# A windowed-attention kernel with top-1 experts: scatters without mutual order, a reordered attention step, and loads on two queues

## The chip, the core and the metric

The kernel runs on one core of a Trainium2 chip. A core has a matrix engine (TensorE, PE), a vector engine (VectorE, DVE), an engine for activations (ScalarE, ACT), a general one (GpSimd, POOL) and SyncE (SP), which here only issues transfers. Each takes its instructions in order from a queue of its own; semaphores join them. Sixteen DMA engines move data for all of them. The metric is device microseconds of one execution, lower is better.

## The reference

Attention with a window of 32 positions to either side and eight global positions, over 8 batches of 8 heads, 576 positions of 64; then a layer of eight experts, each token going to one:

```
scores = scale * np.matmul(q, k.transpose(0, 1, 3, 2))
mask = np.abs(pos[:, None] - pos[None, :]) <= window
mask = mask | is_global[:, None] | is_global[None, :]
...
x = attn_out.transpose(0, 2, 1, 3).reshape(B * S, H * D)
logits = x @ w_gate
expert_idx = np.argmax(logits, axis=1)
...
for e in range(E):
    h = np.maximum(x[expert_idx == e] @ w1[e], 0.0)
    out[expert_idx == e] = gate_w[expert_idx == e, None] * (h @ w2[e])
```

## The kernel before

The order on each engine is that of the source, written out by hand (a manual schedule); a framework places the semaphores from what each instruction reads and writes. There are four stages.

*Setup.* q, k and v of batch 0 are loaded (`load_qk`, L136; `load_v`, L145, twelve transfers of 96 KB a batch), all from SP. GpSimd gathers the k, q and v rows of the global positions with 16 indirect transfers (L202, L207), then makes identity and masks. q and k are cast to 16 bits and transposed on TensorE (`cast_qk`, L283; `trans_qk`, L289); the global v rows are copied into the v tiles (`load_vg`, L152).

*Attention.* `for b in range(B)`, and in it six steps t of 48 rows in each half of the sequence. A step consists of `scores` (a mask matmul, L357, then L370), `exps` (ScalarE, L377), `pvs` (P·V, L388), `zs` (the softmax sums, L400), and `merge_x` and `merge_z` (L405), which add the 12 columns that overlap with the step before on VectorE (L415), copy the 8 new ones on ScalarE (L410) and sum the columns of the global queries (L417). The scores of the next step are computed ahead of the present one's last merge. Between the steps stand two other kinds of work: casts (GpSimd, at the start of batch b), transposes of q and k of batch b + 1, and the `Tail` of batch b − 1. A tail computes router logits (`gate`, L458; `logits`, L473), normalized 16-bit rows (`rows`, L494), the choice of expert and the slot (`route1`, `ranks`, `route2`), and at t = 5 writes the rows into a slot table in DRAM with six indirect transfers (`scatter`, L571). Tail pieces and transposes share a pool of two PSUM tiles (tag `tr`). After the last step `join` (GpSimd, L430) adds the seams of the two halves in place. In batches 1 to 4 two pieces of expert weights of 1 MB are loaded and cast on ScalarE at t = 3 and 4 (L590).

*End of attention.* The tail of batch 7, and one for the global rows of all batches (`tg`), run with nothing beside them, then seven scatters.

*Experts.* For each of eight: four blocks of 128 rows are gathered from the slot table (`gather`, L712, with a memset on VectorE ahead of it, L711), transposed (L732), multiplied by w1 (L832), passed through a ReLU on ScalarE and VectorE in turn (L747, L749), multiplied by w2 (L850), scaled (`yout`) and scattered to the output by indirect transfers (L742). Eight row buffers serve two experts. Weights come in pieces of 1 MB through two staging buffers (`wfetch`, L582, L585), and are cast on GpSimd, VectorE and ScalarE (L592, L590). `overflow_plan`, some 30 small VectorE operations in expert 1, works out which blocks are left over where an expert has more than 512 tokens; these run last, one by one (`ov_block`).

The framework orders all writes to the slot table among each other, and all writes to the output, since it can't see that the indices differ.

## Time and profile before

| | |
|---|---|
| median of three runs | 799.98 us (799.2 to 801.22) |
| the profiled execution | 797.85 us, span 795.8 |
| busy in the span: PE, PEld | 416.0, 251.0 us |
| busy: DVE, ACT, POOL | 260.1, 170.8, 230.6 us |
| mean granted TensorE clock | 0.794 of 2.4 GHz |
| moved by DMA | 83.91 MB, mean 105 GB/s |

PE is TensorE's matmuls, PEld its weight loads. "[18.79 <-POOL wall L283]" means that the engine was idle for 18.79 us before the instruction, and that the wait ended with what line 283 did on POOL. L and a number is a line of the kernel; a `q` behind an engine's name is its queue, where transfers are issued. A clock of 1.00 is 2.4 GHz, 0.50 is 1.2 GHz. Tiles carved out of the weights' memory all go by the name `wall`.

### The profile page before, as it was taken

How to read it: one execution, taken by the hardware profiler on the slowest of the kernel's cores; microseconds unless marked ns; L12 is line 12 of the kernel's file. 1: busy time of each engine (PE TensorE's matmuls, PEld its weight loads, DVE VectorE, ACT ScalarE, POOL GpSimd, SP SyncE). 2: the span in 40 equal slices, each digit the busy share in tenths (PEclk: the TensorE clock that was granted, in tenths of full speed). 3: DMA queues.
4: the chain of work that ended last, by engine and by line, in shares of the span. 5: the costliest groups of instructions: out<-in, count | busy, mean ns of one | idle time of the engine just before them, and what ended most of it. 6: DMA issues, size and time to landing. Idle time of an engine off the chain costs nothing. (4 is left out here: it accounts for less than half of the span.)

```text
span 795.8 us, 15839 instructions
## 1 busy us (share of the span) xinstructions
PE 416.0 (52%) x6583; PEld 251.0 (32%) x6583; DVE 260.1 (33%) x788; ACT 170.8 (21%) x270; POOL 230.6 (29%) x299
## 2 busy tenths in 40 slices
PE   0036874372572761753735423092763844769774
PEld 0024653251351540541523302041321421324331
DVE  1332253152251450440533424142522331423331
ACT  0033334142241250321221200021202202202121
POOL 5412211502503304116021031334143452543211
PEclk9999698587685785885886856587878868879998
DMA  9069584292471660820000000353636735421100
GB/s 189 11 131 172 88 224 87 60 234 41 103 196 39 157 144 27 161 42 20 2 16 17 7 25 20 143 169 135 227 112 213 255 125 208 166 66 69 65 23 28
DMA packets 74508, 83.91 MB, mean 105 GB/s; under 512 B 43772, under 2 KB 56716, under 8 KB 74432
## 3 DMA queue, kind: packets, MB, share of 16 engines
q1 hardware_dynamic: 64880, 63.46, 32.3%
q0 software_dynamic: 9008, 19.37, 7.5%
q8 instruction: 54, 0.88, 0.5%
q14 instruction: 22, 0.18, 0.1%
q10 hardware_dynamic: 544, 0.02, 0.0%
HBM read 68.10 MB, written 16.16 MB: 106 GB/s over the span
## 5 line engine op out<-in xcount | busy, mean ns | idle before, releaser
L832 PE MATMUL h<-xts,wall 128*128 128x512 f16 x256 | 71.8, 438 | 71.0 <-DVE ht L747 61.2
L289 PE MATMUL tr_qk<-idh,wall 96*128 96x96 f16 x384 | 28.0, 228 | 136.9 <-POOL wall L283 92.3
L388 PE MATMUL pv<-wall 56*64 56x128 f32 x1536 | 71.9, 336 | 22.6 <-issue 11.1
L571 POOL DMA_INDIRECT xslot_scr<-wall,si x25 | 24.9, 995 | 160.5 <-DVE wall L565 117.5
L388 PEld LDWEIGHTS pv<-wall 56*64 56x64 f32 x1536 | 56.5, 168 | 37.3 <-issue 19.1
L571 POOL DMA_INDIRECT xslot_scr<-x16x,si x24 | 23.8, 994 | 148.8 <-DVE x16x L565 90.5
L742 POOL DMA_INDIRECT out_dram<-y,xr x32 | 31.8, 993 | 116.3 <-DVE y L741 35.6
L289 PEld LDWEIGHTS <-wall 96*128 96x128 f16 x384 | 21.0, 109 | 140.0 <-POOL wall L283 93.0
L832 PEld LDWEIGHTS <-wall 128*128 128x128 f16 x256 | 27.6, 108 | 111.7 <-issue 89.4
L377 ACT ACTIVATE wall<-sc 128x1024 f32<-128x1024 f32 x48 | 49.1, 1023 | 59.6 <-PE sc L370 59.6
L850 PE MATMUL yp<-wall,ht 128*128 128x512 f16 x256 | 57.2, 381 | 2.4 <-DVE y L741 2.4
L410 ACT ACTIVATE xt<-pv 128x384 f32<-128x384 f32 x48 | 23.5, 490 | 133.2 <-PE pv L388 133.2
L462 DVE SCALAR_TENSOR_TENSOR lsb<-zt,tr_l 128x216 f32<-128x216 f32 x24 | 9.0, 373 | 126.3 <-PE tr_l L458 126.2
L415 DVE TENSOR_TENSOR xt<-xt,pv 128x576 f32<-128x576 f32 x40 | 30.2, 754 | 58.6 <-ACT xt L410 58.5
L749 ACT ACTIVATE ht<-h 128x512 f16<-128x512 f32 x32 | 18.7, 596 | 140.3 <-PE h L832 140.0
L283 POOL CAST wall<-wall 96x768 f16<-96x768 f32 x56 | 43.6, 818 | 8.9 <-DMA wall<-in_q_dram 5.3
L494 PE MATMUL tr_x<-id,xt 128*108 128x128 f32 x192 | 31.4, 313 | 24.2 <-ACT kt L294 22.3
L458 PE MATMUL tr_l<-xt,wgbd 128*32 128x216 f32 x192 | 18.1, 465 | 47.5 <-POOL xt L430 37.2
L400 PE MATMUL z<-wall,onesel 56*32 56x128 f32 x1536 | 40.0, 324 | 5.2 <-issue 5.2
L294 ACT ACTIVATE kt<-tr_qk 128x576 f16<-128x576 f16 x32 | 21.0, 656 | 100.0 <-PE tr_qk L289 100.0
L712 POOL DMA_INDIRECT xr<-xslot_scr,idx x32 | 35.3, 1103 | 16.6 <-issue 8.2
L850 PEld LDWEIGHTS <-ht 128*128 128x128 f16 x256 | 25.0, 99 | 31.4 <-issue 3.2
(225 smaller groups left out, 662.6 us busy)
## 6 DMA issues: line engine op xcount, KB each, us to landing
st<-in_moe_w_dram SPq DMA_DIRECT2D x24, 1024.0 KB
wall<-in_v_dram SPq DMA_DIRECT2D x96, 96.0 KB
wall<-in_moe_w_dram SPq DMA_DIRECT2D x8, 1024.0 KB
wall<-in_k_dram SPq DMA_DIRECT2D x7, 1152.0 KB
wall<-in_q_dram SPq DMA_DIRECT2D x7, 1152.0 KB
wall<-vg SPq DMA_DIRECT2D x16, 96.0 KB
wall<-in_k_dram SPq DMA_DIRECT2D x4, 288.0 KB
wall<-in_q_dram SPq DMA_DIRECT2D x4, 288.0 KB
```

Source lines behind the costliest of these rows:

```text
L283: eng.tensor_copy(o, i_)
L289: nc.tensor.transpose(out=ps[:, 96 * r : 96 * r + 96], in_=src[:, 768 * pair + 128 * r : 768 * pair + 128 * r + 128], identity=idh[0:96, 0 ...
L377: nc.scalar.activation(out=e.rearrange("p r c w -> p r (c w)"), in_=sc[:, :, 0 : 4 * WE], func=AF.Exp, scale=0.125)
L388: nc.tensor.matmul(out=pv[64 * r : 64 * r + 64, f, c * WE : (c + 1) * WE], lhsT=vt[ff, t, 64 * h : 64 * h + 64], rhs=e[ff, r, c, :], start ...
L400: nc.tensor.matmul(out=z[32 * c : 32 * c + 32, f, 0:WE], lhsT=onesel[ff, r, :], rhs=e[ff, r, c, :], start=(r == 0), stop=(r == 1))
L415: nc.vector.tensor_tensor(out=dl[:, :, :, o : o + 12], in0=dl[:, :, :, o : o + 12], in1=sl[:, :, :, 0:12], op=ALU.add)
L494: nc.tensor.transpose(out=ps[p, 128 * c : 128 * c + 128], in_=src, identity=id32)
L571: nc.gpsimd.indirect_dma_start(out=xslot, out_offset=IndirectOffsetOnAxis(ap=self.si[p, j : j + 1], axis=0), in_=self.x16[p, j, :].bitcast ...
L712: nc.gpsimd.indirect_dma_start(out=xr.bitcast(I16), out_offset=None, in_=xslot, in_offset=IndirectOffsetOnAxis(ap=ix, axis=0), bounds_chec ...
L742: nc.gpsimd.indirect_dma_start(out=out, out_offset=IndirectOffsetOnAxis(ap=xr[:, DM : DM + 2].bitcast(I32), axis=0), in_=y, in_offset=None ...
L832: nc.tensor.matmul(out=ps, lhsT=w1v[:, e, c, 128 * fb : 128 * fb + 128], rhs=xts[:, c, :], start=(c == 0), stop=(c == 3))
L850: nc.tensor.matmul(out=ps, lhsT=ht[:, fc, 128 * j : 128 * j + 128], rhs=w2v[:, e, fc, :], start=(fc == 0), stop=(fc == 7))
```

## The change

In the setup, identity and masks are made ahead of the gathers; twelve gathers replace 16 (v rows for two heads' halves land in 128 partitions and are copied to their place by two transfers), and the copy of the global v rows is issued ahead of the loads of batch 1. Constants of the routing are made after the first exp. Loads of q, and half of the v loads, are issued from ScalarE's queue; q sits in partitions 32 to 127, and its transposes have 128 columns. The columns of the global queries stand first in each block of scores; their sums over the steps are no longer kept by VectorE in each step, but copied by ScalarE with the new columns and added up once per batch (`sum_globals`). `merge_x` works in halves, which the two engines take in opposite order. In the step, the k transposes stand ahead of the scores, tail pieces and q transposes behind the exp in a new order, and the q loads at t = 4. Scatters to the slot table carry no order among each other, those of the output in the experts neither; the first gather waits for all scatters. The six scatters of a batch are issued one batch later, behind the casts. The overflow plan is cut into pieces of five operations between the ReLUs of expert 1. The diff, cut to its core:

```diff
-    def load_qk(b, pieces=1):
-        n = H // pieces
-        for i in range(pieces):
-            for dst, src in ((kf, k), (qf, q)):
-                nc.sync.dma_start(
-                    out=dst[:, 384 * n * i : 384 * n * (i + 1)].rearrange("p (h n) -> p h n", h=n),
-                    in_=src[b, n * i : n * (i + 1)].rearrange("h (p r) d -> p h (r d)", r=6))
+
+    def load_qk(b, which="kq"):
+        for i in range(4):
+            for w, dst, src, eng in (("k", kf, k, nc.sync), ("q", qf[32:128], q, nc.scalar)):
+                if w in which:
+                    eng.dma_start(
+                        out=dst[:, 768 * i : 768 * (i + 1)].rearrange("p (h n) -> p h n", h=2),
+                        in_=src[b, 2 * i : 2 * (i + 1)].rearrange("h (p r) d -> p h (r d)", r=6))
     def load_v(b):
         d = vb[b % 2]
         for t in range(NT):
             for f in range(2):
                 s0 = 288 * f + HW * t
-                nc.sync.dma_start(
+                (nc.scalar if f else nc.sync).dma_start(
                     out=d[64 * f : 64 * f + HW, t, :].rearrange("p (h d) -> p h d", h=H),
                     in_=v[b, :, s0 : s0 + HW, :].rearrange("h s d -> s h d"))
...
+
+    for dst, src in ((vgr, v), (kg, k), (qg, q)):
+        for i in range(4):
+            h = 4 * (i // 2) + i % 2
+            nc.gpsimd.indirect_dma_start(
+                out=dst[:, i, :], out_offset=None, in_=src.rearrange("b h s d -> (b h s) d"),
+                in_offset=IndirectOffsetOnAxis(ap=ridx[:, h : h + 1], axis=0),
+                bounds_check=B * H * S - 1, oob_is_err=False)
+    for s_ in range(2):
+        nc.sync.dma_start(out=vg.rearrange("p (u s r) d -> p u s (r d)", u=2, s=2)[:, :, s_],
+                          in_=vgr[64 * s_ : 64 * s_ + 64].rearrange("p (u r) d -> p u (r d)", u=2))
...
     def trans_qk(b, pair, which):
-        src = k16 if which == "k" else q16
         ps = trp.tile([128, 1024], FP16, tag="tr", name="tr_qk")
         for r in range(6):
-            nc.tensor.transpose(out=ps[:, 96 * r : 96 * r + 96], in_=src[:, 768 * pair + 128 * r : 768 * pair + 128 * r + 128],
-                                identity=idh[0:96, 0:96])
+            sl = slice(768 * pair + 128 * r, 768 * pair + 128 * r + 128)
+            if which == "q":
+                nc.tensor.transpose(out=ps[:, 128 * r : 128 * r + 128], in_=q16[:, sl], identity=idh)
+            else:
+                nc.tensor.transpose(out=ps[:, 96 * r : 96 * r + 96], in_=k16[:, sl], identity=idh[0:96, 0:96])
         if which == "q":
-            nc.vector.tensor_copy(qt[b % 2][:, pair, :, 6:102], ps[:, 0:S].rearrange("p (r a) -> p r a", r=R))
+            nc.vector.tensor_copy(qt[b % 2][:, pair, :, 6:102],
+                                  ps[:, 0:768].rearrange("p (r a) -> p r a", r=R)[:, :, 32:128])
...
-    def merge(t, src, n, dl, dg):
-
-        sl = src[:, :, 0:WQ].rearrange("p n (r a) -> p n r a", r=R)
-        sg = src[:, :, WQ:WE]
+    def merge(t, parts):
+
+
+
         o = 8 * t
-        nc.scalar.activation(out=dl[:, :, :, o + 12 : o + WP], in_=sl[:, :, :, 12:WP], func=AF.Copy)
-        if t == 0:
-            nc.vector.tensor_copy(dl[:, :, :, 0:12], sl[:, :, :, 0:12])
-            nc.vector.tensor_copy(dg, sg)
-        else:
-            nc.vector.tensor_tensor(out=dl[:, :, :, o : o + 12], in0=dl[:, :, :, o : o + 12],
-                                    in1=sl[:, :, :, 0:12], op=ALU.add)
-            nc.vector.tensor_tensor(out=dg, in0=dg, in1=sg, op=ALU.add)
+        new, old = [], []
+        for src, acc in parts:
+
+            sn = bass.AP(src.tensor, src.offset, [list(src.ap[0]), list(src.ap[1]), [WP, R + 1], [1, 8]])
+            new.append((acc[:, :, :, o + 12 : o + WP], sn))
+            old.append((acc[:, :, 1 : R + 1, o : o + 12],
+                        src[:, :, NG:WE].rearrange("p n (r a) -> p n r a", r=R)[:, :, :, 0:12]))
+        for i in range(len(parts)):
+            nc.scalar.activation(out=new[i][0], in_=new[i][1], func=AF.Copy)
+            d_, s_ = old[-1 - i]
+            if t == 0:
+                nc.vector.tensor_copy(d_, s_)
+            else:
+                nc.vector.tensor_tensor(out=d_, in0=d_, in1=s_, op=ALU.add)
 
     def merge_x(b, t, pv):
-        merge(t, pv.rearrange("p f (c w) -> p (f c) w", c=4), 8,
-              xt[b % 2].rearrange("p f c r a -> p (f c) r a"), xg[b % 2].rearrange("p f c g -> p (f c) g"))
+        merge(t, [(pv[:, f].rearrange("p (c w) -> p c w", c=4), xt[b % 2][:, f]) for f in range(2)])
 
     def merge_z(b, t, z):
-        merge(t, z[:, :, 0:WE], 2, zt[b % 2], zg[b % 2])
+        merge(t, [(z[:, :, 0:WE], zt[b % 2])])
...
+    def sum_globals(b):
+        x, z = xt[b % 2], zt[b % 2]
         s_ = slice(8 * b, 8 * b + 8)
-        nc.gpsimd.tensor_tensor(out=xtg[:, 0:4, s_], in0=xg[b % 2][:, 0], in1=xg[b % 2][:, 1], op=ALU.add)
-        nc.gpsimd.tensor_tensor(out=xtg[:, 4, s_], in0=zg[b % 2][:, 0], in1=zg[b % 2][:, 1], op=ALU.add)
+        for f in range(2):
+            nc.vector.tensor_reduce(out=gsum[:, f, 0:4], in_=x[:, f, :, 0, 12:XP].rearrange("p c (t g) -> p c g t", t=NT),
+                                    op=ALU.add, axis=AX.X)
+            nc.vector.tensor_reduce(out=gsum[:, f, 4], in_=z[:, f, 0, 12:XP].rearrange("p (t g) -> p g t", t=NT),
+                                    op=ALU.add, axis=AX.X)
+        nc.vector.tensor_tensor(out=xtg[:, :, s_], in0=gsum[:, 0], in1=gsum[:, 1], op=ALU.add)
...
         def scatter(self):
             p = slice(0, self.np)
             for j in range(self.nj):
-                nc.gpsimd.indirect_dma_start(
+                d_ = nc.gpsimd.indirect_dma_start(
                     out=xslot, out_offset=IndirectOffsetOnAxis(ap=self.si[p, j : j + 1], axis=0),
                     in_=self.x16[p, j, :].bitcast(I16), in_offset=None,
                     bounds_check=E * CAP - 1, oob_is_err=False)
+                tc.declare_no_dep(d_.ins, group="xslot", reason="every token has a slot of its own")
+                tc.add_to_no_dep_group("xslot", d_.ins)
+                scattered.append(d_.ins.name)
...
-    tail = None
+    routing_constants()
+    tail = done = None
     for b in range(B):
         if b + 1 < B:
             load_v(b + 1)
             load_vg(b + 1)
             for pair in range(4):
-                cast_qk(pair, nc.gpsimd)
-            fill_kg(b + 1)
+                cast_qk(pair, nc.gpsimd, nc.gpsimd)
+            fill_kg(b + 1, nc.gpsimd)
             if b + 2 < B:
-                load_qk(b + 2)
+                load_qk(b + 2, "k")
+        if done is not None:
+            done.scatter()
         if 1 <= b <= 7 and pre:
             wl = [pre.pop(0) for _ in range(min(2, len(pre)))]
             for i, p_ in enumerate(wl):
@@ -612,45 +660,53 @@
             wl = []
         for t in range(NT):
             n = NT * b + t
+            tr = t - 1 if b + 1 < B and 1 <= t <= 4 else None
             pv = pvs(b, t)
+            merge_x(b, t, pv)
             z = zs(b, t)
-            merge_x(b, t, pv)
+            merge_z(b, t, z)
+            if tr is not None:
+                trans_qk(b + 1, tr, "k")
             if n + 1 < NT * B:
                 nb, nt = divmod(n + 1, NT)
                 sc = scores(nb, nt)
                 exps(n + 1, sc)
-            merge_z(b, t, z)
-            if b + 1 < B and t < 5:
-                for pos in ((0,), (1,), (2, 3), (4, 5), (6, 7))[t]:
-                    trans_qk(b + 1, pos // 2, "kq"[pos % 2])
             if tail is not None:
-                if t == 0:
-                    tail.gate(0)
-                elif t == 1:
+                if t == 1:
                     tail.logits(0)
-                    tail.gate(1)
                 elif t == 2:
+                    tail.logits(1)
+                elif t == 3:
+                    tail.logits(2)
+                elif t == 4:
+                    tail.rows(1, 0)
+                    tail.ranks()
+                elif t == 5:
+                    tail.rows(2, 0)
+            if tr is not None:
+                trans_qk(b + 1, tr, "q")
+            if tail is not None:
+                if t < 3:
+                    tail.gate(t)
+                elif t == 3:
+                    tail.route1()
                     tail.rows(0, 0)
                     tail.rows(0, 1)
-                    tail.logits(1)
-                    tail.gate(2)
-                elif t == 3:
-                    tail.rows(1, 0)
+                elif t == 4:
                     tail.rows(1, 1)
-                    tail.logits(2)
-                elif t == 4:
-                    tail.route1()
-                    tail.rows(2, 0)
-                    tail.rows(2, 1)
-                    tail.ranks()
                 else:
                     tail.route2()
-                    tail.scatter()
+                    tail.rows(2, 1)
+            if t == 4 and b + 2 < B:
+                load_qk(b + 2, "q")
             if wl and t in (3, 4):
                 wcast(*wl[t - 3], stage[t - 3], nc.scalar)
+        sum_globals(b)
         join(b)
+        done = tail
         tail = Tail(b)
     tg = Tail(B)
+    done.scatter()
...
     def gather(xr, ix):
 
         nc.vector.memset(xr[:, DM : DM + 2].bitcast(I32), 10 ** 6)
-        nc.gpsimd.indirect_dma_start(out=xr.bitcast(I16), out_offset=None, in_=xslot,
-                                     in_offset=IndirectOffsetOnAxis(ap=ix, axis=0),
-                                     bounds_check=E * CAP - 1, oob_is_err=False)
+        d_ = nc.gpsimd.indirect_dma_start(out=xr.bitcast(I16), out_offset=None, in_=xslot,
+                                          in_offset=IndirectOffsetOnAxis(ap=ix, axis=0),
+                                          bounds_check=E * CAP - 1, oob_is_err=False)
+        while scattered:
+            tc.add_manual_dep(d_.ins, scattered.pop(), mybir.DependencyInfo(
+                mybir.DependencyClass.Sync, mybir.DependencyReason.DATA), reason="slots of all tokens")
...
-    def yout(ps, xr, eng):
+    def yout(ps, xr, eng, free=True):
         y = fy.tile([128, DM], FP32, tag="y", name="y")
         g = xr[:, DM + 2 : ROW].bitcast(FP32)
         if eng == "act":
             nc.scalar.activation(out=y, in_=ps, func=AF.Copy, scale=g)
         else:
             nc.vector.tensor_scalar(out=y, in0=ps, scalar1=g, scalar2=None, op0=ALU.mult)
-        nc.gpsimd.indirect_dma_start(out=out, out_offset=IndirectOffsetOnAxis(ap=xr[:, DM : DM + 2].bitcast(I32), axis=0),
-                                     in_=y, in_offset=None, bounds_check=NTOK - 1, oob_is_err=False)
+        d_ = nc.gpsimd.indirect_dma_start(out=out, out_offset=IndirectOffsetOnAxis(ap=xr[:, DM : DM + 2].bitcast(I32), axis=0),
+                                          in_=y, in_offset=None, bounds_check=NTOK - 1, oob_is_err=False)
+        if free:
+            tc.declare_no_dep(d_.ins, group="out", reason="every token has a row of its own")
+            tc.add_to_no_dep_group("out", d_.ins)
...
     def overflow_plan():
         nc.vector.tensor_copy(nbm, nbm_i)
+        yield
         nc.vector.tensor_copy(e8, e8i)
+        yield
         thr = fp.tile([128, NOV], FP32, name="thr")
         nc.vector.tensor_scalar(out=thr, in0=nbm, scalar1=128.0, scalar2=float(BASE), op0=ALU.mult, op1=ALU.add)
...
-        if e == 1:
-            overflow_plan()
+        plan = iter(overflow_plan()) if e == 1 else iter(())
...
+            for _ in range(5):
+                next(plan, None)
```

## Rows read from the trace of the kernel before

**Rows 1.** The page: busy tenths, TensorE and DMA engines, 40 equal slices

```profile
PE   0036874372572761753735423092763844769774
...
DMA  9069584292471660820000000353636735421100
```

**Rows 2.** Waits: engine, line, what for: us in all, times, longest

```profile
PE tr_qk L289 <- POOL wall L283: 92.3, 6, 19.9
...
DVE xr L711 <- DMA out_dram<-y,xr: 83.9, 22, 6.1
...
PE h L832 <- DVE ht L747: 61.2, 6, 18.3
...
PE tr_l L458 <- POOL xt L430: 37.2, 2, 20.0
```

**Rows 3.** Timeline 126 to 160: start, us, engine, line, operation [idle before]

```profile
130.73 1.08 POOL L571 DMA_INDIRECT xslot_scr<-wall,si  x1 [27.65 <-DVE wall L565]
134.37 1.01 POOL L571 DMA_INDIRECT xslot_scr<-wall,si  x1 [2.55 <-DMA xslot_scr<-wall,si]
...
146.27 0.99 POOL L571 DMA_INDIRECT xslot_scr<-wall,si  x1 [1.97 <-DMA xslot_scr<-wall,si]
...
149.01 6.21 POOL L283 CAST wall<-wall 96x768 f16<-96x768 f32 x8
...
149.88 0.66 PE L289 MATMUL tr_qk<-idh,wall 96*128 96x96 f16 x6 [18.79 <-POOL wall L283]
```

**Rows 4.** Stretches: busy PE, PEld, DVE, ACT, POOL; granted clock, DMA share, GB/s

```profile
80.00:93.00 13.00, 11.71 (x246) 8.62 (x248) 3.28 (x10) 4.40 (x8) 0.19 (x1) 0.50 0.62 103
...
98.00:131.00 33.00, 23.89 (x703) 17.36 (x695) 18.24 (x59) 15.06 (x25) 5.35 (x9) 0.95 0.77 177
131.00:150.00 19.00, 0.21 (x14) 0.12 (x3) 0.72 (x4) 1.17 (x2) 8.51 (x14) 0.58 0.15 36
```

**Rows 5.** Timeline: one step without tail; a tail's transpose in batch 1

```profile
70.77 1.10 PE L388 MATMUL pv<-wall 56*64 56x128 f32 x32 [0.79 <-ACT wall L377]
...
73.26 1.02 ACT L377 ACTIVATE wall<-sc 128x1024 f32<-128x1024 f32 x1 [0.81 <-PE sc L370]
...
74.33 1.10 PE L388 MATMUL pv<-wall 56*64 56x128 f32 x32 [0.60 <-ACT wall L377]
...
115.85 1.09 PE L494 MATMUL tr_x<-id,xt 128*108 128x128 f32 x8 [1.28 <-ACT kt L294]
```

**Rows 6.** Timeline of the setup, to the exp of step 1 of batch 0

```profile
25.80 0.94 POOL L207 DMA_INDIRECT vg<-in_v_dram,ridx  x1 [0.30 <-issue]
...
47.66 1.65 SPq L152 DMA_DIRECT2D wall<-vg  x2
...
66.18 1.02 ACT L377 ACTIVATE wall<-sc 128x1024 f32<-128x1024 f32 x1 [1.43 <-PE sc L370]
```

**Rows 7.** Timeline from the end of the last batch to the first gather

```profile
450.55 0.67 PE L400 MATMUL z<-wall,onesel 56*32 56x128 f32 x32
...
471.20 1.67 PE L458 MATMUL tr_l<-xt,wgbd 128*32 128x216 f32 x16 [19.98 <-POOL xt L430]
...
505.81 0.94 POOL L571 DMA_INDIRECT xslot_scr<-wall,si  x1 [2.44 <-DMA xslot_scr<-x16x,si]
...
510.37 1.05 POOL L712 DMA_INDIRECT xr<-xslot_scr,idx  x1 [3.46 <-DVE xr L711]
```

**Rows 8.** Stretches of experts 1, 2 and 7, and the sum of all eight

```profile
536.82:573.06 36.24, 16.63 (x81) 7.56 (x80) 16.42 (x43) 5.56 (x7) 9.96 (x9) 0.76 0.51 172
573.06:601.04 27.98, 17.82 (x82) 8.06 (x81) 7.95 (x16) 4.74 (x7) 10.42 (x9) 0.82 0.50 161
...
718.68:732.49 13.81, 13.81 (x67) 6.33 (x66) 4.27 (x6) 3.76 (x6) 3.94 (x4) 1.00 0.18 67
sum 213.11, PE 137.44 PEld 62.67 DVE 70.03 ACT 39.54 POOL 83.47; mean PE 17.18 PEld 7.83 DVE 8.75 ACT 4.94 POOL 10.43
```

**Rows 9.** The v loads' line: ns of one issue, least/median/most

```profile
L145 SPq DMA_DIRECT2D wall<-in_v_dram x96: 311/678/7085, 6.8 to 348.7; - x96
```

More of the change, by code (lines that the diff above doesn't have):

```diff
@@ L83, with short @@
     stage = [carve(128, 2048, FP32) for _ in range(2)]
+    early = [0]
+    def short(*shape):
+        n = 1
+        for d_ in shape:
+            n *= d_
+        a = early[0]
+        early[0] = a + n
+        assert early[0] <= 2048
+        r = stage[1][:, a : a + n]
+        return r.rearrange("p (a b) -> p a b", b=shape[1]) if len(shape) > 1 else r
     x16b = [carve(TB, 6 * ROW, FP16).rearrange("p (j n) -> p j n", j=6)]
@@ L343 @@
[L343 to L348 removed]
+    fill_kg(0, nc.vector)
+    nc.vector.memset(qt[1][:, :, :, 0:6], 0.0)
+    nc.vector.memset(qt[1][:, :, :, 102:108], 0.0)
```

247 lines of the change are left out of this document (130 added, 117 removed).

## The prediction

> **What bounds the kernel now.** I read the page first, then the list of waits, then the boundary of one batch, then the two ends and the experts. No engine bounds the program: in the slices of the page TensorE falls to a few tenths again and again, and the DMA engines are full in some slices and nearly idle in others [rows 1]. The program is made of four stages in series, each bound by a queue that works in order. The list of waits names three of the four [rows 2]: TensorE's transposes of the next batch's q and k wait 92.3 us in six waits for a cast on GpSimd; the last gates wait 37.2 us in two waits for the joins on GpSimd; and VectorE waits 83.9 us in 22 waits for output scatters to land, behind which TensorE waits 61.2 us for the ReLUs that VectorE can't do meanwhile.
>
> The batch boundary shows why [rows 3]. GpSimd issues the six scatters of a batch one by one, at 130.73, 134.37 and so on up to 146.27, some 3 us apart, because each waits until the one before has landed. Behind them on GpSimd stand the joins and then the eight casts of the next batch (149.01), and TensorE's first transpose waits for the first cast: 18.79 us idle. In that stretch the DMA engines are at 0.15, so nothing else is being waited for [rows 4]. The granted clock there is 0.58, and after a shorter stop it is 0.50 for 13 us (1.2 GHz), against 0.95 in the undisturbed stretch 98 to 131 [rows 4].
>
> **The change part by part.** The sum goes against the profiled execution: 797.85 us, its span of 795.8 and 2.05 outside. It lies 2.1 us under the median of 799.98, which I add at the end.
>
> *Setup, up to the exp of step 1 of batch 0 (66.18 [rows 6]).* Now 16 gathers hold GpSimd until 26.7 (25.80 plus 0.94), and identity, masks, casts and transposes come behind them; the copy of the global v rows is issued at 47.66, behind the next batch's q and k in the same queue, and the first P·V waits for it [rows 6]. After, identity and masks stand ahead of the gathers, the gathers are 12, and the global rows are issued ahead of the next batch. I place the first gather at 7.5 us (my estimate: identity and ten mask selects come before it). Twelve at 1.24 us (0.94 and 0.30 idle) end at 22.4; landing, two transposes, the copies and a fill take some 6 us, scores, exp, P·V, Z and scores again some 5: the same exp at 33. The loads of batch 0 don't hold this up: the first slice of the page shows the DMA engines full for 20 us and then idle [rows 1]. Minus 33 us; between minus 25 (gathers land late) and minus 38.
>
> *The loop.* Deferred scatters: `done.scatter()` stands behind the casts, so that all 129.5 us of the two GpSimd waits [rows 2] lose their cause, whether or not the scatters wait for each other. What is late next is the step itself. A step without tail takes 3.56 us from P·V to P·V (70.77 to 74.33): 2.5 us from the start of P·V over Z and the next scores to the start of the exp (70.77 to 73.26), then the exp with 1.02 [rows 5]. With tail, steps were longer, because pieces that share two PSUM tiles stood in one row after the exp; the tail's transposes wait for the k copy that ScalarE does only after the exp (1.28 us at 115.85 [rows 5]). The stretch 98 to 131 is 33.0 us of such steps, six of them with no GpSimd wait, and TensorE is busy for 23.9, VectorE for 18.2, ScalarE for 15.1 [rows 4]. So a full batch lies between 24 (TensorE never idle) and 37 (33 and a stop of the clock).
>
> The reordering puts the k transpose ahead of the scores (0.34 us more before the exp, in four steps, 1.4 in all) and the logits, rows and gates between other matmuls. It takes two adds for the global columns off VectorE in each step and puts five small sums per batch in their place. It halves the merge, so that ScalarE and VectorE work on opposite halves: some 0.5 us less before the next P·V may write. I credit it with half of the 9.1 us in which TensorE is idle: 33.0 − 4.5. Against that stand the six v loads per batch that ScalarE now issues at the start of a loop, and four q loads at step 4. An issue of a v load on SP took 0.31 to 7.09 us, 0.68 in the median [rows 9]: six take 4.1, of which the 2.3 us of P·V, Z and scores hide about half, so 1.8 are left. One fall of the clock per batch adds 1.7. That makes 33.0 − 4.5 + 1.8 + 1.7 = 32. The q loads at step 4 (four at about 0.4 us) lie beside P·V and are free; without that cover they cost 1.6 per batch. SP loses the q loads and half of v and so reaches the expert weights sooner; the GpSimd queue has joins, casts and scatters for 1.7 + 6.7 + 7.4 = 16 us of 32 (the joins lie between 147.3 and 149.01, the casts take 6.2 [rows 3], the key fill is put at 0.5).
>
> Now the loops run from 66.18 to 451.22 (the end of Z at 450.55 [rows 6, 7]), 385 us. After: batch 0 without a tail 26 (now it has 13 us at half the clock [rows 4]), batches 1 to 6 at 32, batch 7 without transposes and casts 24: 242. Minus 143 us; at 26 per batch minus 180, at 38 minus 105.
>
> The Trainium skill, "DMA: Bandwidth & Descriptors", section "Issuing engines are not separate DMA queues", says that DMAs issued from several engines run on the same 16 engines, and that spreading them saves only the time of issuing, usually small. By it the issue term would be about zero and the forecast 13 us lower; the trace's 0.68 in the median and 7.09 at most say that an issue can hold its engine for longer, and I go by the row.
>
> *The end of attention (451.2 to the first gather at 510.37 [rows 7], 59 us).* The join no longer stands behind six scatters: the gate at 471.20 comes about 3.5 us after Z instead of 20. From there to the gather it is 39.2 us now, in which seven scatters go out 3.5 us apart, the last at 505.81. Unordered they are 1.24 apart: 6 × 2.26 = 13.6 less. Six deferred scatters of batch 6 (7.4 us) lie beside the gates and routing. 3.5 + 39.2 − 13.6 = 29, and 2 for the wait for all of them to land, which falls on the first gather: 31. Minus 28; between minus 20 and minus 32.
>
> *The experts (519.38 to 732.49, 213.1 us [rows 8]).* The last expert, with nothing to prefetch, takes 13.81 us at full clock; one in the middle takes 28, TensorE busy for 17.8 at a clock of 0.82 [rows 8]. Between stand the output scatters, each waiting for the one before, and the memset of the next row buffer on VectorE, which waits for their landing with the ReLUs queued behind it. Unordered, three spacings of 3.5 fall to 1.3, 6.7 us, and GpSimd's weight cast, queued behind the gathers, frees its staging buffer that much sooner, so that the next weights land earlier: 2 to 3 us more. Experts 2 to 5 at 19 (now 28 and more), expert 1 at 26 (now 36; the overflow plan, for which VectorE is busy for 16.4 us instead of 8 [rows 8], is cut into pieces between the ReLUs but keeps its length), expert 6 at 16, expert 0 and 7 as now: 17.4 + 26 + 76 + 16 + 13.8 = 149. Minus 64 us; between minus 40 (weights at the pace of the staging buffers) and minus 80. The overflow blocks behind keep their order and their time.
>
> Sum: 33 + 143 + 28 + 64 = 268; 797.85 − 268 = 530; as a median 532.
>
> **The rivals.** *Everything overlaps better:* batches of 28 and experts of 17 give 24 + 8 less, and the setup a little: 495. For it: TensorE's 23.9 us per batch. Against it: two PSUM tiles for all pieces.
>
> *The order stays* (the scatters still wait for each other, because the same queue or a wait that was not named holds them). The loop keeps its gain, since 1.7 + 6.7 + 18 us on GpSimd fit into 32; the end of attention is 15 longer and the experts keep 213: 532 + 15 + 64 = 611. Against it: the gathers of the setup go out at 0.30 us of idle, with no order, in the same queue [rows 6].
>
> *ScalarE becomes the bound through its issues.* At 2 us per issue the six v loads cost 12 − 2.3 per batch, 7.9 more than counted, and the q loads on the way add a few: 532 + 55 + 10 = 597. For it: the longest issue in [rows 9]. Against it: the median.
>
> *Slower than before, by the same place:* there are 66 such issues on ScalarE in the loops (42 of v, 24 of q), with merges and exps queued behind each. From 268/66 = 4.1 us per issue on, uncovered, the gain is gone; at the longest, 7.09, it would be 532 + 66 × 6.4 = 954. Only the few longest issues on SP are above that price, and those stood behind a full queue.
>
> **How the numbers follow.** The forecast's case 0.62, better overlap 0.15, ScalarE's issues 0.11, the order stays 0.08, slower 0.02, and 0.02 for what I have not seen. The likeliest case's own range is 500 to 570, from the bounds of the parts (they won't all fall to one side). From 485 to 600 the case of ScalarE's issues and the better overlap are in, and about 0.12 is left out. A measurement of this kernel tells about 0.3% from no change: faster by more 0.97, within 0.01, slower 0.02.
>
> **What would show it.** Right: six scatters per batch about 1.3 us apart, no wait of a transpose for a GpSimd cast over 2 us, a clock near 1.0 from 35 us on, exps of step 1 some 32 us apart, output scatters 1.3 apart, and VectorE's wait for them below 30 us. Wrong: v issues on ScalarE's queue of 2 us and more with the exp of step 1 late; scatters still 3 us apart; a clock of 0.5 through whole batches, which makes 40 us of 24 and the forecast 600; weights that land after their cast is due.

## The result and the profile after

The changed kernel takes 579.64 us (median of 4 runs, 574.57 to 584.51) against 800.44 beside it: a ratio of 0.722, 95% interval 0.717 to 0.727. The ratio leaves out the slowest of the four executions (584.51), which counts as a slow one. The profiled execution took 578.62 us, with a span of 576.8. That is faster, as forecast, and inside the range of 485 to 600, but 48 us above the 532 that I named, and 10 us above the 570 that bounded the likeliest case. Read by stages from the two traces, as in the prediction (setup up to the exp of step 1 of batch 0; loops up to the end of the last Z; end of attention up to the first gather; experts from the first h matmul to the end of expert 7):

| stage, us | before | forecast | after |
|---|---|---|---|
| setup | 66.2 | 33 | 40.2 |
| loops | 385.0 | 242 | 264.3 |
| end of attention | 59.2 | 31 | 31.4 |
| experts | 213.1 | 149 | 169.8 |

What is left, between first gather and experts and behind the experts, moved by 1 us. So the end of attention came out as summed, and the other three terms were too hopeful, by 7, 22 and 21 us.

The page of the changed kernel, its slices of TensorE, of the granted clock and of the DMA engines (busy share of 40 slices in tenths; against [rows 1]):

```profile
PE   0368578695896868869785529657876968997772
PEclk9997979799777996978997659878978889999997
DMA  8896894948738575440101155665967755210000
```

The deep holes of before are gone. The granted clock is 0.86 in the loops and 0.90 in the experts; a clock near 1.0 from 35 us on, which I had named as a sign of being right, didn't come. Then the list of waits (engine and line waited, for what: us in all, times, longest), against [rows 2]:

```profile
POOL xt L462 <- DVE xt L449: 170.4, 8, 28.2
...
DVE xr L767 <- DMA out_dram<-y,xr: 48.7, 22, 5.9
...
ACT xt L444 <- DMA wall<-in_v_dram: 37.2, 7, 7.0
...
PE h L914 <- DVE ht L809: 23.1, 6, 5.6
```

TensorE's waits for GpSimd's casts and joins (92.3 and 37.2 us before) are not in it any more; now GpSimd is the one that stands idle, up to 28.2 us in each batch, until the last merge lets it join. VectorE's wait for output scatters fell from 83.9 to 48.7 us, not below 30 as I had forecast. And there is a new row: ScalarE's merge, 37.2 us in seven waits. The boundary between two batches shows what it is (timeline of the changed kernel; start, duration, engine and line, operation, and in brackets the idle time before and its releaser; against [rows 3]):

```profile
99.85 1.02 ACT L403 ACTIVATE wall<-sc 128x1024 f32<-128x1024 f32 x1
99.87 6.27 ACTq L162 DMA_DIRECT2D wall<-in_v_dram  x6
...
101.72 1.10 PE L414 MATMUL pv<-wall 56*64 56x128 f32 x32
101.73 6.21 POOL L280 CAST wall<-wall 96x768 f16<-96x768 f32 x8
101.89 0.71 DVE L602 TENSOR_TENSOR si<-sl,invbig 108x6 int32<-108x6 f32 x1
...
102.86 2.80 DVE L607 COPY wall<-tokt 108x6 int32<-108x6 int32 x1
...
106.19 0.36 ACT L444 ACTIVATE xt<-pv 128x224 f32<-128x224 f32 x1 [5.32 <-DMA wall<-in_v_dram]
...
107.92 0.45 DVE L447 COPY xt<-pv 128x288 f32<-128x288 f32 x1
108.39 0.36 ACT L444 ACTIVATE xt<-pv 128x224 f32<-128x224 f32 x1 [1.85 <-DVE xt L447]
...
108.60 1.07 POOL L613 DMA_INDIRECT xslot_scr<-wall,si  x1 [0.21 <-DVE xt L447]
108.79 1.03 ACT L403 ACTIVATE wall<-sc 128x1024 f32<-128x1024 f32 x1
...
109.98 1.01 POOL L613 DMA_INDIRECT xslot_scr<-wall,si  x1 [0.30 <-issue]
```

P·V of step 0 is done at 102.82. ScalarE begins to merge it only at 106.19, because its queue holds six v issues, 6.27 us long: the releaser's name is that of the transfer, the wait is for ScalarE's own issuing. Then it waits 1.85 us more for VectorE, whose own queue was late: a copy of six numbers per row took 2.80 us while GpSimd casts, and behind it stand the rows (0.69 us) and the five sums of the global columns, which run until the merge begins at 107.92. The next exp starts 8.94 us after the last, in place of the 5.30 us in loop 7, which loads nothing. The scatters behind, some 1.3 us apart, are what was forecast.

Loops 2 and 7 and experts 1, 2, 3 and 7 of the changed kernel in its table by stretches (us, then busy time of PE, PEld, DVE, ACT, POOL with counts, granted clock, DMA share, GB/s; against [rows 4, 8]):

```profile
102.80:137.30 34.50, 26.39 (x720) 18.97 (x719) 22.86 (x60) 16.95 (x31) 14.07 (x20) 0.90 0.74 188
...
284.20:304.50 20.30, 16.87 (x510) 11.83 (x511) 12.36 (x37) 8.96 (x20) 3.96 (x4) 0.92 0.10 27
```

```profile
361.61:391.44 29.83, 18.02 (x82) 8.07 (x81) 16.53 (x44) 6.52 (x8) 10.18 (x10) 0.83 0.61 214
391.44:411.56 20.12, 16.80 (x81) 7.93 (x80) 10.20 (x15) 5.00 (x7) 8.98 (x9) 0.92 0.67 219
411.56:435.36 23.80, 17.56 (x82) 7.79 (x81) 10.00 (x22) 6.12 (x8) 12.90 (x12) 0.86 0.72 258
...
499.90:513.70 13.80, 13.80 (x66) 6.25 (x65) 4.27 (x6) 3.76 (x6) 4.97 (x6) 1.00 0.25 92
```

And the end of attention (timeline; against [rows 7]), from the last gate over the last scatter to the first gather:

```profile
307.20 0.57 PE L500 MATMUL tr_l<-xt,wgbd 128*32 128x216 f32 x8
...
330.45 0.93 POOL L613 DMA_INDIRECT xslot_scr<-wall,si  x1 [0.30 <-issue]
...
335.86 1.06 POOL L768 DMA_INDIRECT xr<-xslot_scr,idx  x1 [3.46 <-DVE xr L767]
```

### The profile page after: what moved, and what is told of

It reads as the page before. It is cut to its first block, busy times and chain, and to the rows that moved or that the text cites. A ratio compares the mean times of both kernels' runs of the same rounds, so it can differ in the third digit from the quotient of the medians.

```text
span 576.8 us, 15876 instructions
## 1 busy us (share of the span) xinstructions
PE 405.5 (70%) x6583; PEld 244.5 (42%) x6583; DVE 291.5 (51%) x779; ACT 179.6 (31%) x318; POOL 223.8 (39%) x279
## 4 chain that ended last, share of the span: by engine, by line
PE 25%; DVE 24%; issue 18%; DMA 18%; ACT 8%; POOL 5%; ACTq 0%; POOLq 0%; DVEq 0%
PE pv L414 8%; DMA out_dram<-y,xr 7%; DMA out_dram<-y,xo 4%; ACT xt L444 3%; DMA wall<-in_v_dram 3%; DVE xt L449 3%; DMA wall<-in_q_dram 3%; PE z L426 3%; PE h L914 2%; POOL out_dram L801 2%; ACT wall L403 2%; DVE wall L537 2%; DMA xr<-xslot_scr,idx 2%; PE tr_l L500 2%; PE tr_x L536 2%
## 5 line engine op out<-in xcount | busy, mean ns | idle before, releaser
L914 PE MATMUL h<-xts,wall 128*128 128x512 f16 x256 | 68.9, 430 | 25.0 <-DVE ht L809 23.1
L444 ACT ACTIVATE xt<-pv 128x224 f32<-128x224 f32 x96 | 34.2, 356 | 137.2 <-PE pv L414 64.7
L462 POOL TENSOR_TENSOR xt<-xt 128x144 f32<-128x144 f32 x16 | 8.1, 507 | 170.4 <-DVE xt L449 170.4
L449 DVE TENSOR_TENSOR xt<-xt,pv 128x288 f32<-128x288 f32 x80 | 36.3, 454 | 72.6 <-ACT xt L444 72.6
L914 PEld LDWEIGHTS <-wall 128*128 128x128 f16 x256 | 27.3, 107 | 63.8 <-issue 40.2
L280 POOL CAST wall<-wall 96x768 f16<-96x768 f32 (+1 forms) x56 | 43.6, 822 | 5.5 <-DMA wall<-in_q_dram 3.4
L536 PE MATMUL tr_x<-id,xt 128*108 128x128 f32 x192 | 33.4, 303 | 15.5 <-DVE wall L537 5.4
L293 PE MATMUL tr_qk<-idh,wall 96*128 96x96 f16 x192 | 16.8, 237 | 21.3 <-ACT wall L278 21.3
L536 PEld LDWEIGHTS tr_x<-id,xt 128*108 128x108 f32 x192 | 21.5, 142 | 22.9 <-DVE wall L537 6.5
L809 DVE TENSOR_SCALAR ht<-h 128x512 f16<-128x512 f32 x32 | 21.6, 688 | 18.9 <-PE h L914 18.9
L791 PE MATMUL tx<-idh,xr 128*128 128x128 f16 x128 | 12.1, 241 | 26.9 <-DMA xr<-xslot_scr,idx 14.5
L798 ACT ACTIVATE y<-yp,xr 128x512 f32<-128x512 f32 x16 | 10.9, 684 | 63.6 <-PE yp L934 62.7
L396 PEld LDWEIGHTS <-kt 64*64 64x64 f16 x1536 | 26.5, 118 | 6.9 <-issue 2.8
```

What stands on the lines that cost most here:

```text
L280: eng.tensor_copy(o, i_)
L396: nc.tensor.matmul(out=o[:, NG:WE].rearrange("p (r a) -> p r a", r=R) if part == 0 else o[:, 0:NG], lhsT=kt[b % 2][rr, c, sl, :], rhs=rhs, ...
L444: nc.scalar.activation(out=new[i][0], in_=new[i][1], func=AF.Copy)
L449: nc.vector.tensor_tensor(out=d_, in0=d_, in1=s_, op=ALU.add)
L536: nc.tensor.transpose(out=ps[p, 128 * c : 128 * c + 128], in_=src, identity=id32)
L914: nc.tensor.matmul(out=ps, lhsT=w1v[:, e, c, 128 * fb : 128 * fb + 128], rhs=xts[:, c, :], start=(c == 0), stop=(c == 3))
```

## The experiments

The theory at the start: the 22 us of the loops lie in ScalarE's v issues, the 21 us of the experts in the memset of a row buffer that waits for the landing of an output scatter. Rivals: the DMA engines set both paces. The stages of all runs, read as above from the profiled execution (time: the median of all executions; the profiled one lies 8 us above it in tok_only, 5 above in before_free, and 3 to 4 below in rows12, out_ordered and step_before):

| kernel | time, us | setup | loops | end | experts |
|---|---|---|---|---|---|
| A: v_on_sp | 600.7 | 37.1 | 284.7 | 31.4 | 175.5 |
| A: v_spread | 605.8 | 43.2 | 283.0 | 31.4 | 176.6 |
| A: rows12 | 594.1 | 41.6 | 287.9 | 33.4 | 154.1 |
| A: out_ordered | 652.2 | 41.7 | 288.3 | 32.3 | 211.9 |
| B: after_again | 578.35 | 39.4 | 259.0 | 31.4 | 172.7 |
| B: v_sp_tok | 560.5 | 36.9 | 245.3 | 31.1 | 175.6 |
| B: combo | 531.8 | 37.1 | 235.0 | 32.2 | 154.5 |
| B: no_defer | 606.8 | 39.9 | 280.1 | 39.3 | 173.0 |
| C: x_ordered | 606.65 | 44.9 | 267.5 | 48.0 | 170.9 |
| C: before_free | 688.5 | 66.5 | 338.8 | 38.2 | 176.5 |
| C: step_before | 649.0 | 41.7 | 329.5 | 30.5 | 171.6 |
| C: tok_only | 607.2 | 42.1 | 291.7 | 31.2 | 177.2 |

A, B and C are the groups run together, each on one chip. The kernel before took 798 to 801 in all of them, but loops that carry the changed kernel's code unaltered take 288 in group A (rows12, out_ordered) and 259 to 264 in group B and in the first profile. The last section shows what was different. I therefore compare stages with the same stage of kernels of the same group that did not alter it. The times expected of group A were worked out from the first profile, and miss by some 24 us for this alone.

**v on SP.** `(nc.scalar if f else nc.sync).dma_start(` becomes `nc.sync.dma_start(`.

> All v loads are issued by SP again, in the setup and in the loops; everything else is as in the changed kernel (579.6 us). Theory, ScalarE is held by its six v issues at the start of each loop (5.3 to 6.3 us in the trace, with the merges of step 0 and the next exp behind them): the exp of step 1 then follows that of step 0 after about 5.5 us in loops 0 to 6, as it does in loop 7, where no loads are issued (5.30), in place of 8.1 to 9.4. Seven loops at some 3.4 us are 24 us, and the setup gains 3 to 5 by the first cast on ScalarE: about 553 us, between 545 and 562. Rival, the DMA engines set the pace of the issues and whoever issues them only moves the wait: P.V waits for v, or the weights on SP come later, and the time stays between 573 and 585.

Loops 284.7 against 288 in its group, setup 37.1 against 41.6: 8 us, not 24. The first step of loop 1 fell to 3.7 us, as the theory had it, but those of loops 2 to 6 stayed at 8 to 9. The rival isn't seen either: no P·V of the loops waits for v, and the casts wait 18.5 us for weights, against 15.8 in v_spread. Timeline of this kernel at the same boundary:

```profile
93.36 6.24 POOL L280 CAST wall<-wall 96x768 f16<-96x768 f32 x8
...
95.31 2.01 DVE L607 COPY wall<-tokt 108x6 int32<-108x6 int32 x1
95.42 3.76 SPq L153 DMA_DIRECT2D wall<-in_k_dram  x4
95.43 0.36 ACT L444 ACTIVATE xt<-pv 128x224 f32<-128x224 f32 x1 [1.98 <-PE pv L414]
...
99.58 0.45 DVE L447 COPY xt<-pv 128x288 f32<-128x288 f32 x1
100.06 0.36 ACT L444 ACTIVATE xt<-pv 128x224 f32<-128x224 f32 x1 [4.27 <-DVE xt L447]
```

ScalarE is there at 95.43, and then waits 4.27 us for VectorE. With one wait gone, the next one, which had run beside it, set the same end. At the boundary ahead of loop 1 no routing runs yet, so that VectorE isn't late there, and the whole gain shows.

**The issues spread.** One v load of ScalarE behind the exp of each step:

```
                exps(n + 1, sc)
+            if b + 1 < B:
+                load_v(b + 1, (t,), (1,))
```

> The six v loads of ScalarE go out one per step, behind that step's exp, in place of six in a row at the start of the loop; the setup is as in the changed kernel. Theory, the issues hold ScalarE because six follow each other into a queue that is still working on the one before (0.32 us where the queue was empty, about 1 us apart in a row): alone each takes 0.3 to 0.5 us, the first step of each loop falls to about 5.8 us, and the time to 560 us (555 to 568). Rival, each such issue costs ScalarE about 1 us wherever it stands: the first steps fall, but the others grow by 0.5 to 1 us each, and the time stays between 574 and 585.

The issue of a v load on ScalarE, all 48 of this kernel (shortest, median, longest ns):

```profile
L162 ACTq DMA_DIRECT2D wall<-in_v_dram x48: 317/318/406, 5.0 to 293.3; - x48
```

In the changed kernel the same line reads 317/483/1966. So the price belongs to six in a row at the start of a loop, and the rival's 1 us wherever it stands is out. The loops came to 283.0, 5 less, with the same 9.0 us first steps in loops 2 to 6 (3.7 in loop 1): VectorE again.

**Twelve row buffers.** `name="fxr", bufs=8` becomes `bufs=12`.

> Twelve row buffers for the experts in place of eight, so that a gather takes a buffer whose output scatter was issued an expert earlier. Theory, what holds the experts above my forecast is the landing of the output scatters (4 to 6 us beside the weight loads), because the memset of the next row buffer on VectorE waits for it with the ReLUs behind it (48.7 us in 22 waits): the wait falls below 10 us, the experts 2 to 5 go from 20.1 to 23.8 us down to 17 to 19, the experts together from 169 to about 148, and the time to 559 (553 to 566). Rival, the weights set the pace through their two staging buffers: the wait goes, but VectorE and GpSimd then wait for weights instead, the experts stay above 162 together and the time above 573.

The experts take 154.1 against 175.5 and 176.6 in the group, and VectorE's wait for output scatters is gone altogether. Experts 2 to 6 take 20.1 to 20.6 us rather than the 17 to 19 of the theory, which had 148 for all eight: weights are now waited for (15.3 us in eight waits), so the rival holds for the rest. Expert 1 falls from 31.5 to 21.2 us, although its overflow plan is unaltered: the plan was not what made it long.

**Output scatters ordered.** `free=True` becomes `free=False`.

> The output scatters of the experts wait for each other again, all else as in the changed kernel. Theory, the experts' gain (213 us before, 169 after) comes from the missing order alone: the scatters stand over 3 us apart again, the experts together take 205 to 215 us and the time is about 620 us (612 to 630). Rival, a good part comes from the overflow plan, now cut into pieces between the ReLUs, and from SP reaching the weights earlier: the experts take 185 to 200 us and the time is 596 to 611.

211.9 us against 176: the 36 us are the missing order's, and the experts are back at the 213 of before. With the order in place the cut plan and the earlier weights are worth next to nothing.

**The changed kernel again.**

> The changed kernel itself, beside the others of this group. In the runs before, pieces that two kernels share took longer than in the first profile of the changed kernel (loops 2 to 6: 38.6 to 39.8 us in place of 34.5). If that belongs to the machine of that group, this kernel comes out near 605 us there and near 580 elsewhere; if the edits had made the loops longer, it comes out at 580 beside edits that take longer.

578.35: 579.64 is no matter of chance. The changed kernel itself wasn't run on the chip of group A; that the longer loops there are the group's rests on rows12 and out_ordered, whose loops are unaltered.

**The token copy off the boundary, v on SP.** The copy in `route2` stands in `logits(0)` instead:

```
+            if i == 0:
+                nc.vector.tensor_copy(self.x16[p, 0 : self.nj, DM:ROW].bitcast(I32)[:, :, 0], ...
...
-            nc.vector.tensor_copy(self.x16[p, 0:J, DM:ROW].bitcast(I32)[:, :, 0],
-                                  tokg if self.glob else tokt[:, b, :])
```

> v loads on SP alone, and the copy of six token numbers per row, which stood in route2 at the loop's boundary, moved to step 1. With the loads on SP alone the first steps of loops 2 to 6 kept their 8 to 9 us, and the wait named was one of ScalarE for VectorE. Theory, VectorE is late there because that copy takes 2.0 to 2.8 us beside GpSimd's eight casts of q and k (0.13 us in the kernel before, where no cast ran beside it), and the merge of step 0 stands behind it: with both causes gone the first steps take 5.5 to 6.5 us, 2.5 to 3 less in each of loops 2 to 6, and the time is 14 to 22 us below the changed kernel's own in this group. Rival, VectorE's queue is late for its own length (routing, rows and five sums ahead of the merge): the first steps stay above 8 us and the time within 6 us of the changed kernel's.

560.5, 17.9 less, inside the theory's 14 to 22; first steps of 6.3 to 6.6 us, against its 5.5 to 6.5. The copies took 0.14 to 0.37 us at their new place. Two causes went together here; how the 17.9 divide between them the run doesn't tell.

**Both causes and the experts'.** In addition the sums of the global columns behind the merges of step 0, and twelve row buffers:

```
             merge_z(b, t, z)
+            if t == 0 and b > 0:
+                sum_globals(b - 1)
```

> v loads on SP, the token copy at step 1, the sums of the global columns behind the first merges of the next loop, and twelve row buffers for the experts. Theory: the first steps of loops fall to about 5.3 us as in loop 7, which is 3.5 us in each of seven loops, and the experts take 154 us as with twelve row buffers alone, against 176: together 40 to 50 us below the changed kernel's own time in this group. Rival, the pieces that are moved off the boundary lengthen the next steps by as much: only the experts' 20 us and the setup's 3 are left, 20 to 27 us.

531.8 us (531.55 to 536.53), 46.6 less: a ratio to the kernel before of 0.668, interval 0.665 to 0.672. This version beats both. First steps are 4.5 to 4.8 us (loop 1: 3.7), loops 24 and experts 18 us shorter than in after_again. Of the loops' 24 us, 10 came between v_sp_tok and this run, with the five sums moved: beside the issues and the copy, the sums were a third cause of the late boundary. ScalarE's wait for VectorE at the merge of step 0, first in this kernel, then in v_on_sp (lists of waits):

```profile
ACT xt L444 <- DVE xt L447: 5.2, 8, 0.9
```

```profile
ACT xt L444 <- DVE xt L447: 27.4, 8, 5.2
```

**Scatters not deferred.** `tail.scatter()` at the end of step 5, `done.scatter()` gone.

> The six scatters stand at the end of their own loop again, ahead of the joins and casts on GpSimd, but without mutual order, all else as in the changed kernel. Theory, order and place both count: six scatters 1.3 us apart are 7.8 us on GpSimd ahead of the casts, the k transpose of step 1 then waits for its cast 3 to 6 us, in six loops 20 to 35 us together, partly covered by the v issues: 10 to 30 us above the changed kernel's own time in this group. Rival, the missing order alone clears the boundary, and the place of the scatters is worth nothing: within 5 us.

28.5 us more, at the upper end of the theory's range, and the rival is out; but it stands at another place than I had named: not the transposes, the gates wait, since the joins stand behind six scatters.

```profile
PE tr_l L500 <- POOL xt L462: 53.4, 7, 9.8
```

**Slot scatters ordered.** The two no-order declarations in `Tail.scatter` are taken out.

> The scatters of the rows to the slots wait for each other again, but keep their place behind the casts; all else as in the changed kernel. Theory, in the loops the place alone is enough: joins, casts and six ordered scatters take some 1.7 + 6.7 + 21 us of GpSimd in a loop of 34, so the loops stay as they are, and only the end of attention grows, where 13 scatters stand in a row after the last gate: 13 to 27 us more, a time of 592 to 606. Rival, the ordered scatters fill GpSimd's queue so far that the next joins and casts come late: the k transpose of step 1 waits over 2 us per loop, and the time is above 620.

606.65, just above the theory's 592 to 606. Loops 267.5, 3 to 8 us more than in the two profiles of the changed kernel, which are of other chips: with the scatters at their new place, the missing order is worth little in the loops. The end grew by 16.6 us (the setup is 3 us longer than others of the group too, for which I have no reason). In its own group this kernel is no slower than tok_only with unordered scatters (607.2), whose loops have the bursts of the last section; the changed kernel wasn't run there. The scatters there wait for each other's landing again:

```profile
345.31 1.00 POOL L613 DMA_INDIRECT xslot_scr<-x16x,si  x1 [2.55 <-DMA xslot_scr<-x16x,si]
348.84 0.99 POOL L613 DMA_INDIRECT xslot_scr<-x16x,si  x1 [2.53 <-DMA xslot_scr<-x16x,si]
```

**The kernel before, without order.** The same declarations put into the kernel before.

> The kernel before (800 us) with nothing changed but the mutual order of the scatters, those to the slots and those to the output. Theory, order is the larger part of each stall: the transposes' wait at the boundary falls from 16.6 to 19.9 us to some 5 in six loops (80 less), the end of attention by 14, the experts by about 40: 665 us (645 to 690). Rival, the place of the scatters ahead of joins and casts is what holds TensorE, and unordered they still hold it for over 10 us: 700 us or more.

688.5, at the upper end of the theory. The experts lost 37 us, the end 21, the loops 46 where the theory had 80. The transposes' wait for casts fell from 92.3 to 37.8 us, but the bursts of the last section came in, as waits of the exp for something that the profile names only remote, 35.0 us:

```profile
ACT wall L377 <- remote: 35.0, 6, 8.3
...
PE tr_qk L289 <- POOL wall L283: 37.8, 5, 9.9
```

**The step's order as before.** Merges, k transposes and tail pieces where they stood, all else as changed.

> The changed kernel with the order within a step as it was before: merges behind Z and the exp, the k and q transposes and all tail pieces in one row behind the exp, logits and gates in the steps where they stood; scatters, casts, loads and the split merges as in the changed kernel. Theory, the order within the steps is worth what I credited it with, 4 to 5 us a loop: 25 to 35 us more, 603 to 615. Rival, it is worth nothing beside the waits at the boundary of the loops: within 6 us of 579.

Loops 329.5 against 288 in the kernels of group A, which have such bursts too: 41 us, above the 25 to 35 that I had credited. Against tok_only in its own group it is 38 us, and 42 in the time. The timeline of a step shows why: the PSUM tiles are passed on in one row behind the exp.

```profile
135.78 0.50 PE L291 MATMUL tr_qk<-idh,wall 128*128 128x128 f16 x6
...
137.50 1.09 PE L536 MATMUL tr_x<-id,xt 128*108 128x128 f32 x8 [1.22 <-ACT kt L298]
...
138.93 0.43 PE L515 MATMUL tr_lt<-id,lsb 128*108 128x128 f32 x2 [0.35 <-DVE x16x L537]
139.29 1.91 PE L414 MATMUL pv<-wall 56*64 56x128 f32 x32
```

**The token copy alone.** As in v_sp_tok, with the v loads left on ScalarE.

> Only the copy of the token numbers is moved from the boundary to step 1; the v loads stay on ScalarE. Theory, the boundary has two waits that run beside each other, ScalarE's six issues (6.3 us) and VectorE's slow copy: with the copy gone ScalarE's wait for VectorE of 1.9 us behind the issues goes, the first steps fall from 9.0 to about 7.1 us, and the time by 9 to 13 us, to about 568. Rival, the copy is the whole of it: the first steps fall to 6.5 us as with the v loads on SP, the time to 563 or less. Other rival, the issues are the whole of it: the first steps stay at 9 us and the time within 4 us of the changed kernel's.

First steps fell from 9.0 to 6.8 to 8.4 us, about as the theory had it, but second steps were 9.7 to 11.0 us long with bursts in them, and the loops (291.7) are no shorter than 288. The profiled execution lies 8 us above the median, too. The run doesn't decide how much the copy is worth by itself.

## Why the prediction was right, and where it was 48 us off

The four parts and their mechanisms were the right ones, but the time lies outside the 500 to 570 of the case that I held likeliest. It lies in the stated range because that took in the rival "ScalarE becomes the bound" (597), and this one is only half of what happened.

*Setup: minus 33 forecast, minus 26 measured.* Identity, masks and gathers came as placed (first gather at 8.67 us, forecast 7.5). The "scores, exp, P·V, Z and scores again some 5" was mis-sized: the two exps are 8.1 us apart, ScalarE being held by six v issues, 6.01 us from the first to the last. With v on SP the step still took 8.0 (in combo P·V waits 3.2 us for the copy of the global v rows, and takes 1.98 us against 1.10 later), and the setup gained 2 to 4.5 us.

*Loops: minus 143 forecast, minus 121 measured.* Deferral did what the sum said: both waits for GpSimd are gone. The reordering did more (38 to 41 us, on chips with bursts, where I had 4.5 in each of seven loops). The 1.7 us for one fall of the clock per batch stood without a working, but held: the second step, at a granted clock of 0.50 behind 5.3 us in which TensorE was idle, mostly takes 5.97 us, and 4.1 to 4.3 in four of the same five loops of combo. Two steps failed. The issue term, 1.8 us per batch, took the median of 0.68 us of a queue that had been SP's alone and let half of it be covered; the trace shows 6.27 us for six. The rival "ScalarE becomes the bound" had the place right and the price at twice what it was. That the longest issues on SP "stood behind a full queue" no row shows. The Trainium skill, "DMA: Bandwidth & Descriptors", "Issuing engines are not separate DMA queues", says that the time to issue is usually small beside the transfer itself. The trace agrees for an issue that stands alone (0.32 us, against 5.8 in the median until a v load has landed); but six in a row took 6.27 us together, and what their engine had to do meanwhile was late by that. The second was not in the sum at all, the length of VectorE's queue at the boundary: without scatters ahead of them the casts come right at the boundary, where the routing ends, and a copy that took 0.13 us before took 2.0 to 2.8. In no_defer, where the scatters hold the casts back again, the copies of all eight batches take 0.13 us; in step_before, with the scatters deferred and the step's order as before, five take 0.75: the deferral made the copy slow, and the reordering made it slower. The five sums, which I had counted only as what replaces two adds per step, stand behind it and ahead of the merge. I costed GpSimd's casts by their own time, not by what they do to VectorE. With issues, copy and sums taken away the loops take 235.0 us. The forecast without its issue term (12.6) would be 229: as a sum the rest was sound to 6 us.

*End of attention: minus 28 forecast, minus 28 measured.* The gate comes 2.7 us after Z, scatters are 1.3 us apart. x_ordered puts 16.6 us on the order, forecast 13.6 to 15.

*Experts: minus 64 forecast, minus 43 measured.* The spacing of the scatters fell as forecast, to 1.3 to 1.7 us, but I let the wait for their landing go with it. It doesn't: they land in 4.5 us in the median (of the few whose landing the trace has) where it was 2.8 before; whether the weight loads beside them or their own neighbours make it so wasn't tried. The memset of the next row buffer stands on VectorE ahead of the ReLUs (48.7 us; TensorE waits 23.1 behind them). Twelve buffers take that wait away, and the experts are at 154, 5 above the forecast. Part of that is luck: experts 2 to 6 stayed longer than I had them, for the weights, and expert 1 came to 21.2 us where I had 26, for a plan that didn't hold it up.

The rival "the order stays" (611) is out by the 1.3 us. "Everything overlaps better" (495) counted on batches of 28 us; they are 32 to 39, and 27.8 to 33.6 in combo. The rival of the order had put 64 + 15 us on it; out_ordered and x_ordered cost 36 + 17. That combo ends at 531.8, beside my 532, is coincidence: it has changes that the forecast didn't count.

## What to carry to other kernels

Before a short VectorE operation is moved, look at what GpSimd does at its new place, and before DMA issues are given to a computing engine, count them as a row and see which merge or exp stands behind. Where two queues are late at the same boundary, taking one wait away can show next to nothing (3 us of the loops with v on SP): the trace names only the later one, and the gain comes with the second. A buffer that is freed by a scatter's landing needs a spare set: here the unordered scatters were issued sooner, but took 4.5 us to land instead of 2.8.

## What the runs showed of the hardware that I had not expected

*VectorE beside GpSimd.* The copy's rows, in the changed kernel and at its new place in v_sp_tok (shortest, median, longest ns):

```profile
L607 DVE COPY wall<-tokt x4: 131/2404/2800, 102.9 to 307.9; 108x6 int32<-108x6 int32 x4
```

```profile
L514 DVE COPY wall<-tokt x4: 166/167/268, 65.5 to 266.9; 108x6 int32<-108x6 int32 x4
```

The copy of 108 x 6 numbers takes 131 ns at its shortest and 2.80 us beside the casts; an addition with two inputs in SBUF (L602) takes 0.17 and 0.71, while the reduction and the reciprocal beside the same casts keep their 0.19 us. The Trainium skill, "SBUF — State Buffer", "Who interferes with whom", says that a copy in a two-port mode contends with GpSimd for a shared pair of ports, which the first to issue has for its whole instruction, that an operation with two SBUF inputs contends with one of GpSimd that reads SBUF, and that reductions on this chip never do. These rows agree as to which operations are slow. The rule alone doesn't say how long: one cast takes some 0.8 us, and each of the five slow copies lasts until the third or fourth cast that it meets has ended, and ends 0.03 us behind it. Why a copy waits for more than one cast, and in which mode it runs, the trace doesn't show.

*Bursts.* In groups A and C TensorE's matmuls came in small groups some 0.7 us apart while unordered slot scatters went out. Scores of loop 7 in rows12, then the same in the changed kernel's first profile:

```profile
301.36 0.22 PE L396 MATMUL sc<-qgt,kt 64*64 64x8 f16 x4 [0.46 <-issue]
302.11 0.24 PE L396 MATMUL sc<-qt,kt 64*64 64x120 f16 x2 [0.53 <-issue]
302.82 0.24 PE L396 MATMUL sc<-qt,kt 64*64 64x120 f16 x2 [0.47 <-issue]
```

```profile
282.63 0.22 PE L396 MATMUL sc<-qt,kt 64*64 64x120 f16 x4
282.69 0.17 PE L396 MATMUL sc<-qgt,kt 64*64 64x8 f16 x4
282.71 0.23 PE L396 MATMUL sc<-qt,kt 64*64 64x120 f16 x4
```

Nothing that the profile shows is waited for. It made 4 to 5 us per loop, 24 to 29 us a run; group B and the first profile have none of it, and in group C x_ordered, whose scatters are 3 us apart, has second steps of 5.4 to 6.4 us where tok_only has 9.7 to 11.0. x_ordered has one loop of 39.8 us among its 35, but no such groups in its scores. That points to the unordered scatters as a condition, on some chips; what holds TensorE then wasn't tried and stays open. The changed kernel may so take some 25 us more on such a chip; neither it nor the improved version was run on one.
